# Long convolutions beside an MLP on TensorE: two blocks of 1024 with 32 by 32 point transforms in place of one 64 by 32 transform of 2048, and a new pacing

## The chip, the cores and the metric

The kernel runs on one core of a Trainium2 chip. The metric is device time in microseconds (us) of one execution, as a median over runs; lower is better. The program is a forward and backward pass with two branches on the same normalised input: a gated MLP and a long convolution. TensorE does the matrix products of both, VectorE and ScalarE the element-wise work, and one engine, SyncE, issues nearly all DMA transfers (1041 of 1121 in the kernel before).

## The reference, cut to what matters

```python
# branch A: k_shift = short causal filter of k (4 taps); kv = k_shift * v
kv_f = rfft(pad(kv, L=4096)); kf_f = rfft(pad(ssm_k, L=4096))   # per channel, 1024 channels
y = irfft(kv_f * kf_f)[:2048] + kv * ssm_D
out_A = q * y                                                    # q = layernorm(x)
# branch B: gated MLP, F = 3584
out_B = (relu(x @ W_gate) * (x @ W_up)) @ W_down
# result: x + out_A + out_B, and by autodiff the gradients of all inputs for a given grad_out
```

Per group of 128 channels automatic differentiation turns this into three forward transforms (filter H, gradient G, kv K), three products in the spectrum and three return transforms. There are eight groups.

## The kernel before

Each transform of 2048 points is made of a first stage R over 64 points, a 32 by 32 transpose on VectorE ("flip"), and a second stage FW over 32 points with the twiddles in its weights. The way back is IA, flip, RB. ScalarE copies each result from PSUM, where the matmuls put it, to SBUF, where the next stage reads it.

```python
def fwd1(self, st, key, src):                      # first stage, R
    B = st[key] = self.big.tile([P, 64, 2, 16, 2], BF16, name="B", tag="big")
    for r0 in range(0, 16, 8):
        for j in range(r0, r0 + 8, 4):
            ps = self.ps.tile([P, 2, 4, P], F32, name="ps1", tag="aps")      # pool of 2 buffers
            for u in range(2):
                rows = slice(64 * u, 64 * u + 64)
                self.mm(ps[:, u]..., self.R[rows]..., src[rows, j:j + 4, :]...)   # 64x128 of the array
            self.act(B[:, :, :, j:j + 4, :], ps[:]...)
        yield
# ... inv_b, the last stage, RB:
            for jj in range(2):
                for u in range(2):
                    n0 = 16 * u + 8 * j + 4 * jj
                    self.mm(ps[64 * u:64 * u + 64, 512 * jj:512 * jj + 512],
                            self.RB[:], Cf[:, n0:n0 + 4, :]...)                  # 128x64 of the array
# ... the product in the spectrum, per half:
            self.tt(t1[:], X[:, g], Z[:, g], ALU.mult)                 # 2048 elements
            self.tt(t2[:, 0], X[:, g, 0], Z[:, g, 1], ALU.mult)        # 1024 each
            self.tt(t2[:, 1], X[:, g, 1], Z[:, g, 0], ALU.mult)
            self.tt(Q[:, g, 0], ...); self.tt(Q[:, g, 1], ...)
```

The convolution is a list of small steps, each at most one burst of matmuls, one piece of VectorE work, or one set of loads. They are woven into the MLP by a budget in nanoseconds of MLP matmul time:

```python
SLOT = 1760
# in steps():
            for p, d in self.slots(st, gi):       # p: a burst or a set of loads; d: VectorE work
                self.run(p); self.run(d)
                yield self.SLOT
# among the slots: next_1 loads the next group's filter, gradient and xn; next_2 its k, v and taps
# the driver, after each run of eight MLP matmuls (ns = 1730):
                left -= ns * pace
                while a_steps is not None and left <= 0:
                    d = next(a_steps, None)
                    ...
                        left += d
```

In the MLP's hidden layer the weights of the next block of 512 columns are fetched late in the current one, into buffers that the current block has just left (cut):

```python
            def gate_up(sp):
                for s in (sp, sp + 1): gate(s); yield from step()
                if end: load_gate()                 # four DMAs of 256 KB, on SyncE
                for s in (sp, sp + 1): up(s); yield from step()
                if end: load_up()
```

Of the kernel before, what the change touches and what calls it, by code (L numbers as in the profile page):

```python
# [48 lines left out]
class ABranch:  # L49
# [5 lines left out]
    def __init__(self, tc, pri, S, D, k, v, g, shift_k, ssm_k, ssm_D, xn_d, y_d, sk_d, out_gk, out_gv, out_gsk,  # L55
                 out_gh, out_gsD):
        assert S == 2048 and D % P == 0
        self.tc, self.nc, self.pri = tc, tc.nc, pri
        self.S, self.D, self.NG = S, D, D // P
        self.k, self.v, self.g, self.shift_k, self.ssm_k, self.ssm_D = k, v, g, shift_k, ssm_k, ssm_D  # L60
        self.xn_d, self.y_d, self.sk_d = xn_d, y_d, sk_d
        self.out_gk, self.out_gv, self.out_gsk, self.out_gh, self.out_gsD = out_gk, out_gv, out_gsk, out_gh, out_gsD
        self.pools, self.pin = [], False
# [51 lines left out]
    def tables(self):  # L115
# [5 lines left out]
        self.IA = con.tile([P, 16, 2, 2, NB1], BF16, name="IA")  # L121
        self.R = con.tile([P, 2, 2, NB1], BF16, name="R")
        self.RB = con.tile([P, 64], BF16, name="RB")
        self.gs_all = con.tile([P, self.NG, 4], F32, name="gs_all")
        self.gD_all = con.tile([P, self.NG], BF16, name="gD_all")
# [20 lines left out]
        n1 = pbit(63, 1.0, "n1p")  # L146

        def first(n, name):
            it = self.ts.tile([P, 2, 2, NB1], I32, name="it" + name, tag="ts")
            tr = self.ts.tile([P, 2, 2, NB1], F32, name="tr" + name, tag="ts")  # L150
            nc.gpsimd.iota(it[:], pattern=[[128, 2], [0, 2], [4, NB1]], base=1, channel_multiplier=0)
            for a in range(2):
                V.tensor_scalar(out=it[:, :, a, :], in0=it[:, :, a, :], scalar1=n[:], scalar2=64.0 * (1 + a) + 128.0,
                                op0=ALU.mult, op1=ALU.add)
            V.tensor_single_scalar(out=it[:], in_=it[:], scalar=255, op=ALU.bitwise_and)
            nc.scalar.activation(out=tr[:], in_=it[:], func=ACT.Sin, scale=TWO_PI / 256, bias=negpi[:])
            return tr

        V.tensor_copy(out=self.R[:], in_=first(n1, "R")[:])

        e128 = con.tile([P, 1], F32, name="e128")
        V.scalar_tensor_tensor(out=e128[:], in0=b64[:], scalar=128.0, in1=b5[:], op0=ALU.mult, op1=ALU.mult)
        itF = big.tile([P, NB1, NB1], I32, name="itF", tag="big")
        nc.gpsimd.iota(itF[:], pattern=[[4, NB1], [256, NB1]], base=1, channel_multiplier=0)
        for ri in range(2):
            off = lin(b32, -2048.0, 2048.0 * (1 + ri) + 4096.0, "offF%d" % ri)
            V.tensor_tensor(out=off[:], in0=off[:], in1=e128[:], op=ALU.add)
            q = big.tile([P, NB1, NB1], I32, name="qF", tag="big")
            V.tensor_scalar(out=q[:], in0=itF[:], scalar1=b5[:], scalar2=off[:], op0=ALU.mult, op1=ALU.add)
            V.tensor_single_scalar(out=q[:], in_=q[:], scalar=8191, op=ALU.bitwise_and)  # L170
            nc.scalar.activation(out=self.FW[:, :, ri, :], in_=q[:], func=ACT.Sin, scale=TWO_PI / 8192,
# [4 lines left out]
        k256 = lin(b5, 256.0, 0.0, "k256")  # L176
        V.scalar_tensor_tensor(out=q32[:], in0=q32[:], scalar=32.0, in1=k256[:], op0=ALU.mult, op1=ALU.add)
        wI = con.tile([P, 16, 1], F32, name="wI")
        itW = con.tile([P, 16, 1], I32, name="itW")
        nc.gpsimd.iota(itW[:].rearrange("p (e m) o -> p e (m o)", e=2), pattern=[[128, 2], [4, 8]], base=1,  # L180
                       channel_multiplier=0)
# [5 lines left out]
        prod = big.tile([P, 16, NB1], F32, name="prI", tag="big")  # L187
        V.tensor_tensor(out=prod[:], in0=wI[:].to_broadcast([P, 16, NB1]), in1=itN[:].to_broadcast([P, 16, NB1]),
                        op=ALU.mult)
        q = big.tile([P, 3, 16, NB1], I32, name="qI", tag="big")  # L190
        for z in range(3):
            V.tensor_scalar(out=q[:, z], in0=prod[:], scalar1=2048.0 * z + 4096.0, scalar2=None, op0=ALU.add)
        V.tensor_single_scalar(out=q[:], in_=q[:], scalar=8191, op=ALU.bitwise_and)
        for ri in range(2):
            for a in range(2):
                nc.scalar.activation(out=self.IA[:, :, ri, a, :], in_=q[:, 1 - a + ri], func=ACT.Sin,
                                     scale=TWO_PI / 8192, bias=negpi[:])

        kk = con.tile([P, 1], F32, name="kkB")
        k4 = lin(b5, 4.0, 1.0, "k4")  # L200
        V.scalar_tensor_tensor(out=kk[:], in0=b64[:], scalar=128.0, in1=k4[:], op0=ALU.mult, op1=ALU.add)
        ob = lin(b32, 64.0, 192.0, "obB")
        itB = con.tile([P, 64], I32, name="itB")
        nc.gpsimd.iota(itB[:], pattern=[[1, 64]], base=0, channel_multiplier=0)
        V.tensor_scalar(out=itB[:], in0=itB[:], scalar1=kk[:], scalar2=ob[:], op0=ALU.mult, op1=ALU.add)
        V.tensor_single_scalar(out=itB[:], in_=itB[:], scalar=255, op=ALU.bitwise_and)
        trB = con.tile([P, 64], F32, name="trB")
        nc.scalar.activation(out=trB[:], in_=itB[:], func=ACT.Sin, scale=TWO_PI / 256, bias=negpi[:])
        V.tensor_scalar(out=self.RB[:], in0=trB[:], scalar1=1.0 / 2048, scalar2=None, op0=ALU.mult)
# [37 lines left out]
    def load_filter(self, gi):  # L247
        cg = slice(gi * P, (gi + 1) * P)
        hn = self.ld.tile([P, 64, NB1], BF16, name="hn")
        for ch in range(2):  # L250
            c0 = gi * P + 64 * ch
            self.load(hn[64 * ch:64 * ch + 64], self.ssm_k[c0:c0 + 64, :].rearrange("c (q n) -> q c n", n=NB1))
# [64 lines left out]
    def fwd1_filter(self, st):  # L317

        B = st["Bh"] = self.big.tile([P, 2, 32, NB1, 2], BF16, name="B", tag="big")
        hn = st["hn"]  # L320
        for k0 in range(0, 4, 2):
            for k in range(k0, k0 + 2):
                ps = self.ps.tile([P, 2, 512], F32, name="ps0", tag="aps")
                for ch in range(2):
                    rows = slice(64 * ch, 64 * ch + 64)
                    self.mm(ps[:, ch], self.R[rows].rearrange("p e a l -> p (e a l)"),
                            hn[rows, 16 * k:16 * k + 16, :].rearrange("p c n -> p (c n)"))
                self.act(B[:, :, 8 * k:8 * k + 8],
                         ps[:].rearrange("p h (cp i n) -> p h cp n i", i=2, n=NB1))
            yield  # L330

    def add_D(self, st):
        for rows in (slice(0, 32), slice(64, 96)):
            b0 = st["Bh"][rows].rearrange("p h cp n i -> p (h cp) n i")[:, :, 0, :]
            self.tt(b0, b0, st["sD"][rows].rearrange("p (cp i) -> p cp i", i=2), ALU.add)

    def fwd1(self, st, key, src):
        B = st[key] = self.big.tile([P, 64, 2, 16, 2], BF16, name="B", tag="big")
        for r0 in range(0, 16, 8):
            for j in range(r0, r0 + 8, 4):  # L340
                ps = self.ps.tile([P, 2, 4, P], F32, name="ps1", tag="aps")
                for u in range(2):
                    rows = slice(64 * u, 64 * u + 64)
                    self.mm(ps[:, u].rearrange("p r c -> p (r c)"), self.R[rows].rearrange("p e a l -> p (e a l)"),
                            src[rows, j:j + 4, :].rearrange("p r c -> p (r c)"))
                self.act(B[:, :, :, j:j + 4, :], ps[:].rearrange("p u r (cp i) -> p cp u r i", i=2))
            yield

    def fwd2(self, st, key, flp):
        F, Bf = self.form(key), st[flp]  # L350
        st[key] = F
        for j0 in range(0, 4, 2):
            for j in range(j0, j0 + 2):
                ps = self.ps.tile([P, 2, 2, 2, P], F32, name="ps2", tag="aps")
                for ri in range(2):
                    for m in range(2):
                        for q in range(4):
                            for e in range(2):
                                rows, l = slice(64 * e, 64 * e + 64), 8 * q + 2 * j + m
                                self.mm(ps[32 * q:32 * q + 32, e, ri, m, :], self.FW[rows, l, ri, :], Bf[rows, l, :])  # L360
                self.act(F[:, 2 * j:2 * j + 2].rearrange("p e i c -> p (e i c)"),
                         ps[:].rearrange("p e i m c -> p (e i m c)"))
            yield

    def form(self, name):
        return self.frm.tile([P, 8, 2, 256], BF16, name=name, tag="frm")

    def cmul(self, st, x, z, conj, name):

        X, Z = st[x], st[z]  # L370
        Q = st[name] = self.form(name)
        for hf in range(2):
            g = slice(4 * hf, 4 * hf + 4)
            t1 = self.tmp.tile([P, 4, 2, 256], BF16, name="t1", tag="tmp")
            t2 = self.tmp.tile([P, 2, 4, 256], BF16, name="t2", tag="tmp")
            self.tt(t1[:], X[:, g], Z[:, g], ALU.mult)
            yield
            self.tt(t2[:, 0], X[:, g, 0], Z[:, g, 1], ALU.mult)
            yield
            self.tt(t2[:, 1], X[:, g, 1], Z[:, g, 0], ALU.mult)  # L380
            yield
            self.tt(Q[:, g, 0], t1[:, :, 0], t1[:, :, 1], ALU.add if conj else ALU.subtract)
            yield
            self.tt(Q[:, g, 1], t2[:, 0], t2[:, 1], ALU.subtract if conj else ALU.add)
            yield

    def inv_a(self, st, key, q_name):
        C = st[key] = self.big.tile([P, 64, 4, 8, 2], BF16, name="C", tag="big")
        Q = st[q_name]
        for j0 in range(0, 4, 2):  # L390
            ps = [self.ps.tile([P, 2, 2, 2, P], F32, name="ps3", tag="aps") for _ in range(2)]
            for j in range(2):
                for m in range(2):
                    for ri in range(2):
                        for q in range(4):
                            for e in range(2):
                                rows, x = slice(32 * q, 32 * q + 32), 8 * e + 2 * (j0 + j) + m
# [1081 lines left out]
```

## Time and profile before

| | before |
|---|---|
| median time | 1908.5 us of four runs (1907.3 to 1910.3) |
| TensorE busy | 1895.0 us, 100% of the span |
| VectorE / ScalarE busy | 48% / 32% |
| convolution's bursts on TensorE | 192, costing 141.3 us |

A row of a group has line, engine, operation, out<-in, shape and count, then busy us and mean ns of one, then the engine's idle time before them and what ended it. A row of the timeline has start and length in us. "PEld" is TensorE's loading of weights into the array, not from memory. The prediction shows the lines themselves.

### The profile page before, as it was taken

To read this page: it belongs to the slowest core of one execution; us is meant where nothing else is said; L and a number is where in the kernel's file an instruction comes from. 1 tells how busy PE (TensorE), PEld (TensorE's weight loads), DVE (VectorE), ACT (ScalarE), POOL (GpSimd) and SP (SyncE) were. 2 spreads that over 40 slices of the span, in tenths; PEclk is the share of its full clock that TensorE was granted. 3 is DMA by queue.
4 is the path that set the end of the run, shared out by engine and by line. 5 is a ranking of instruction groups with operands and counts; after the bars stand their busy time and mean duration, and the time that the engine had idled before them with its cause. 6 is when DMAs were issued, how large, how long until landed. Compare 5 with 4: busy or idle time off the path is not lost.

```text
span 1904.1 us, 36029 instructions
## 1 busy us (share of the span) xinstructions
PE 1895.0 (100%) x15447; PEld 871.9 (46%) x15447; DVE 910.1 (48%) x1355; ACT 618.2 (32%) x858; POOL 15.0 (1%) x37
## 2 busy tenths in 40 slices
PE   9999999999999999999999999999999999999999
PEld 4444444444444444444444444444444544444444
DVE  6667777777777764454354445400222232222222
ACT  5755445445345445344344354311000000000000
POOL 1000000000000000000000000000000000000000
PEclk9999999999999999999999999999999999999999
DMA  9897679877577773566562633394999964554553
GB/s 251 247 226 163 169 185 212 184 202 164 143 200 163 204 208 114 147 157 200 132 170 95 159 112 122 112 290 130 267 237 244 234 142 122 122 122 122 122 122 72
DMA packets 692641, 323.14 MB, mean 170 GB/s; under 512 B 524024, under 2 KB 663040, under 8 KB 692480
## 3 DMA queue, kind: packets, MB, share of 16 engines
q1 hardware_dynamic: 681984, 299.99, 63.4%
q10 hardware_dynamic: 9216, 16.65, 2.8%
q0 software_dynamic: 1280, 4.20, 0.6%
q8 instruction: 120, 1.97, 0.4%
q14 instruction: 41, 0.34, 0.1%
HBM read 143.79 MB, written 95.44 MB: 126 GB/s over the span
## 4 chain that ended last, share of the span: by engine, by line
PE 97%; DVE 1%; DMA 1%; issue 0%; SPq 0%; ACT 0%; DVEq 0%; ACTq 0%
PE ps_x L1336 20%; PE ps_w L1109 20%; PE ps_o L1267 10%; PE ps_h L852 10%; PE ps_u L852 10%; PE ps_g L852 9%; PE ps_d L1109 9%; PE ps L72 6%; PE ps_d L1122 1%; PE ps_w L1122 1%; DMA wg<-in_B_W_gate_dram 0%; PE ps_r L1297 0%; DMA wu<-in_B_W_up_dram 0%; SPq L88 0%; DVE ru L956 0%
## 5 line engine op out<-in xcount | busy, mean ns | idle before, releaser
L1109 PE MATMUL ps_w<-ugs,xn_nat 128*128 128x512 bf16 x1728 | 383.3, 379 | 0.0
L852 PEld LDWEIGHTS <-xnT 128*128 128x128 bf16 x1792 | 170.3, 98 | 209.8 <-issue 9.1
L1109 PEld LDWEIGHTS <-xn_nat 128*128 128x128 bf16 x1728 | 164.6, 98 | 200.6 <-issue 7.6
L852 PE MATMUL ps_g<-wg,xnT 128*128 128x512 bf16 x896 | 206.3, 379 | 1.5 <-ACT xnT L887 0.4
L852 PE MATMUL ps_u<-wu,xnT 128*128 128x512 bf16 x896 | 206.9, 379 | 0.0
L852 PE MATMUL ps_h<-wdT,goT 128*128 128x512 bf16 x896 | 205.6, 379 | 0.0
L1354 ACT ACTIVATE w<-xn,m 128x512 f32<-128x512 bf16 x32 | 24.3, 806 | 553.0 <-issue 317.2
L1336 PE MATMUL ps_x<-wgT,ggT 128*128 128x512 bf16 x896 | 198.6, 379 | 0.0
L1336 PE MATMUL ps_x<-wuT,guT 128*128 128x512 bf16 x896 | 198.6, 379 | 0.0
L1267 PE MATMUL ps_o<-wd,hT 128*128 128x512 bf16 (+1 forms) x896 | 187.6, 372 | 0.0
L1109 PE MATMUL ps_d<-g_nat,hs 128*128 128x512 bf16 x768 | 172.1, 379 | 0.0
L1336 PEld LDWEIGHTS <-guT 128*128 128x128 bf16 x896 | 87.7, 98 | 105.7
L1336 PEld LDWEIGHTS <-ggT 128*128 128x128 bf16 x896 | 87.7, 98 | 105.5
L314 DVE STREAM_TRANSPOSE flp<-C 128x1024 f32<-128x1024 f32 x48 | 90.1, 1934 | 91.8 <-ACT C L76 91.8
L1267 PEld LDWEIGHTS <-hT 128*128 128x128 bf16 x896 | 87.7, 98 | 99.9
L852 PEld LDWEIGHTS <-goT 128*128 128x128 bf16 x896 | 85.0, 98 | 104.7 <-issue 5.8
L956 DVE SCALAR_TENSOR_TENSOR ru<-ru,ps_u 128x512 bf16<-128x512 bf16 x112 | 76.6, 684 | 107.3 <-issue 45.1
L1025 ACT CAST gh<-ps_h 128x512 bf16<-128x512 f32 x112 | 65.5, 584 | 171.3 <-PE ps_h L852 162.9
L1213 ACT CAST wi<-ps_w 128x512 bf16<-128x512 f32 x108 | 63.7, 590 | 162.6 <-PE ps_w L1109 156.6
L76 ACT CAST C<-ps 128x1024 bf16<-128x1024 f32 x96 | 92.5, 1015 | 70.1 <-PE ps L72 68.9
L1109 PEld LDWEIGHTS <-hs 128*128 128x128 bf16 x768 | 72.3, 98 | 89.6 <-issue 5.9
L1338 DVE CUSTOM_DVE_ANT_0 gx<-ps_x,gy 128x512 f32<-128x512 f32 x32 | 22.1, 691 | 182.3 <-PE ps_x L1336 182.2
(160 smaller groups left out, 1495.2 us busy)
## 6 DMA issues: line engine op xcount, KB each, us to landing
ug_d<-ru SPq DMA_DIRECT2D x112, 256.0 KB
ugs<-ug_d SPq DMA_DIRECT2D x112, 256.0 KB
wg<-in_B_W_gate_dram SPq DMA_DIRECT2D x56, 256.0 KB
wu<-in_B_W_up_dram SPq DMA_DIRECT2D x56, 256.0 KB
h_d<-ht SPq DMA_DIRECT2D x112, 128.0 KB
hs<-h_d SPq DMA_DIRECT2D x56, 256.0 KB
out_dram<-wi SPq DMA_DIRECT2D x56, 256.0 KB
gt<-in_grad_out_dram SPq DMA_DIRECT2D x32, 256.0 KB
```

Of the source, the lines that this page charges most:

```text
L72: self.pri.pin(self.nc.tensor.matmul(out, lhsT=lhsT, rhs=rhs, start=start, stop=stop))
L76: self.pri.pin(self.nc.scalar.copy(out=out, in_=in_))
L314: self.pri.pin(self.nc.vector.transpose(out=df[:, c0:c0 + 32, :], in_=sf[:, c0:c0 + 32, :]))
L852: self.pri.pin(self.nc.tensor.matmul(ps[:], lhsT=xT[:, kt * P:(kt + 1) * P], rhs=w(kt), start=(kt == 0), stop=(kt == self.DT - 1)), always ...
L956: self.pri.pin(nc.vector.scalar_tensor_tensor(out=ru[s][:, 1, :], in0=ru[s][:, 0, :], scalar=0.0, in1=ps[:], op0=ALU.is_gt, op1=ALU.mult))
L1025: self.pri.pin(nc.scalar.copy(out=gh[:], in_=ps[:]))
L1109: self.pri.pin(self.nc.tensor.matmul(ps[:], lhsT=lhsT(st), rhs=rhs(st), start=(st == 0), stop=(st == self.ST - 1)))
L1122: self.pri.pin(self.nc.tensor.matmul(ps[i][:], lhsT=lhsT(i, st), rhs=rhs(i, st), start=(st == 0), stop=(st == self.ST - 1)))
L1213: self.pri.pin(nc.scalar.copy(out=wo[0][:, d, :], in_=ps[:]))
L1267: nc.tensor.matmul(ps, lhsT=hT[:, kt, :], rhs=self.wd[:, kt, oc], start=(kt == 0), stop=(kt == self.FT - 1))
L1336: nc.tensor.matmul(ps, lhsT=T[:, kt, :], rhs=W[:, kt, oc], start=(i == 0), stop=(i == n - 1))
L1354: nc.scalar.activation(out=w[:, oc], in_=xn[:, oc], func=ACT.Identity, scale=m[:, 7:8], bias=m[:, 6:7])
```

## The change

The intent is to split each transform of 2048 into two blocks of 1024, so that the first and the last stage have 32 points where they had 64. Their matmuls then fit smaller tiles of the array, eight of which can work side by side (in the kernel before, the first eight matmuls of each FW burst, on 64 by 32 tiles, start within 24 ns). The two blocks are put together again in the spectrum, which costs VectorE more work ("turn" and a longer product). The pacing was changed with it. The core, with cuts:

```diff
-    SLOT = 1760
+    SLOT, DENSE = 1900, (1760, 1250)
...
-                yield self.SLOT
+                yield self.DENSE[p is None] if self.dense else self.SLOT   # dense: after the hidden layer
...
 def fwd1
-            for j in range(r0, r0 + 8, 4):
-                for u in range(2):
-                    rows = slice(64 * u, 64 * u + 64)
-                    self.mm(ps[:, u]..., self.R[rows] (64x128), src[rows, j:j + 4, :]...)
+            for u in range(2):
+                for b in range(2):
+                    rows = slice(64 * u + 32 * b, 64 * u + 32 * b + 32)
+                    for h in range(2):
+                        self.mm(ps[64 * h:64 * h + 64, b], self.R[rows] (32x64), src[rows, r0:r0 + 8, 64 * h:64 * h + 64])
 def inv_b
-                    self.mm(ps[64 * u:64 * u + 64, 512 * jj:512 * jj + 512], self.RB[:] (128x64), ...)
+            for q in range(4):
+                for e in range(2):
+                    rows, n0 = slice(64 * e, 64 * e + 64), 16 * (q // 2) + 8 * j
+                    self.mm(ps[32 * q:32 * q + 32, e], self.RB[rows, e, :] (64x32), ...)
+def turn: two additions of 1024 elements, in place, on the spectra G and H
 def cmul, per half
+                self.tt(t[i][:], M0, N[:, g, :, ::-1] if i else N[:, g], ALU.mult)      # 2048, twice
+                self.tt(u[:], M[:, g, 1], N[:, g, e, ::-1] if i else N[:, g, e], ALU.mult)
+                self.tt(t[i][:, :, f], t[i][:, :, f], u[:], ALU.add)                    # 1024, twice each
...
 def load_filter: four loads of 128 KB per group in place of two of 256 KB
 def store_gh: two stores of the filter's gradient per group in place of one
```

## The prediction

> **What bounds the kernel now.** I read the page of the profile first, its busy shares and its forty slices:
>
> ```profile
> PE 1895.0 (100%) x15447; PEld 871.9 (46%) x15447; DVE 910.1 (48%) x1355; ACT 618.2 (32%) x858; POOL 15.0 (1%) x37
> ...
> PE   9999999999999999999999999999999999999999
> ...
> DVE  6667777777777764454354445400222232222222
> ...
> PEclk9999999999999999999999999999999999999999
> ```
>
> TensorE is busy for 1895.0 of 1904.1 us, in every slice, at full granted clock. The time is therefore a sum of matmul time, and a change moves it in two ways only: by taking matmul time away, or by making TensorE wait. VectorE matters only through the second. The chain of waits says the same (PE 97% of the span). Its share "PE ps L72 6%" is the convolution: line 72 is the helper that issues its matmuls, in bursts between those of the MLP.
>
> I then split line 72 by form (columns: count, busy us, mean ns, idle before):
>
> ```profile
> L72 PE MATMUL ps<-flp,FW 64*32 64x128 bf16 x3072 | 36.2, 221 | 0.5 <-DVE flp L314 0.5
> ...
> L72 PE MATMUL ps<-flp,RB 128*64 128x512 bf16 x128 | 16.9, 385 | 0.0
> ...
> L72 PE MATMUL ps<-GKV,IA 32*64 32x128 bf16 x1024 | 12.4, 224 | 0.0
> ...
> L72 PE MATMUL ps<-gt,R 64*128 64x512 bf16 x64 | 9.7, 381 | 0.0
> ```
>
> "64*128" is the part of the array that one matmul takes (rows by columns). The forms 64*32 and 32*64 put eight matmuls side by side, 64*128 and 128*64 only two. The R form stands three times (inputs gt, kvt, hn). To price a burst I used the timeline, of one first-stage (R) and one last-stage (RB) burst:
>
> ```profile
> 133.45 1.90 PE L852 MATMUL ps_g<-wg,xnT 128*128 128x512 bf16 x8
> 135.28 0.61 PE L72 MATMUL ps<-gt,R 64*128 64x512 bf16 x4
> 135.82 3.63 PE L852 MATMUL ps_u<-wu,xnT 128*128 128x512 bf16 x16
> ...
> 196.20 2.54 PE L852 MATMUL ps_u<-wu,xnT 128*128 128x512 bf16 x11
> 198.66 1.05 PE L72 MATMUL ps<-flp,RB 128*64 128x512 bf16 x8
> 199.65 3.19 PE L852 MATMUL ps_h<-wdT,goT 128*128 128x512 bf16 x14
> ```
>
> MLP matmuls start 0.216 us apart (the median of consecutive starts in the trace), so the eighth of the first run started at 133.45 + 7 x 0.216 = 134.96. The next MLP matmul starts at 135.82. Less the one step of 0.216 that would have passed anyway, the burst costs 0.64 us. In the same way the RB burst costs 199.65 - 198.36 - 0.216 = 1.07 us. Over all bursts of a kind the medians are: R 0.633 us (48 bursts of 4 matmuls), RB 1.080 us (16 of 8), FW 0.776 us (48 of 64), IA 0.785 us (48 of 64). With the tap sums (8.8 us), the filter's last stage (7.4 us) and the halo (1.3 us) all 192 bursts cost 141.3 us; the rest of the 1904 is the MLP, which the change does not touch.
>
> The individual starts within a burst say what that cost is made of. In an R burst they are at 0, 3, 226 and 229 ns, with the last MLP start at -312 and the next at 538: two matmuls together, two more when these are through (about 216), and about 95 ns lost at the switch on either side. In an RB burst they are at 0, 3, 240, 243, 456, 459, 672, 675: four turns of two.
>
> [...] The trace has 3 to 4 ns: the first eight of an FW burst start at 0, 3, 6, 10, 13, 16, 20, 23, and the same holds for most IA bursts. This is the step on which the gain rests: eight tiles of 64*32 or 32*64 really run together here. [...] The trace agrees for plain operands (1216 ns for 2048 elements, 683 for 1024). The changed kernel reverses and repeats middle dimensions only, so I expect the same durations; no run here shows that form yet.
>
> **The change part by part.** The burst count stays at 192 in the built program, so no mode switch is saved.
>
> (a) First stage. A block of 1024 has 32 points where 64 stood, so R goes from 64*128 to 32*64: eight matmuls of 512 columns per burst in place of four, each in its own tile (four row groups by two column groups[...]). All eight should start within 24 ns. Cost: 309 into the burst + 24 + 308 out - 216 = 425 ns against 633. Saved: 48 x 0.208 = 10.0 us. The filter's bursts have the same form.
>
> (b) Last stage. RB goes from 128*64 to 64*32: sixteen matmuls per burst on eight tiles, two turns in place of four. Last start at about 229 + 24 = 253 ns. Cost: 309 + 253 + 308 - 216 = 654 against 1080. Saved: 16 x 0.426 = 6.8 us.
>
> (c) FW, IA and the filter's last stage keep count and size; only their access patterns change. 0.
>
> (d) VectorE gets more work, since the recombination is done in the spectrum. Rows used:
>
> ```profile
> L314 DVE STREAM_TRANSPOSE flp<-B 128x1024 f32<-128x1024 f32 x48 | 90.7, 1937 | 37.4 <-ACT B L76 37.0
> ...
> L80 DVE TENSOR_TENSOR t<-H,G 128x1024 bf16<-128x1024 bf16 x32 | 20.9, 683 | 0.0
> ...
> L80 DVE TENSOR_TENSOR t<-H,G 128x2048 bf16<-128x2048 bf16 x16 | 19.4, 1213 | 31.5 <-ACT G L76 31.5
> ```
>
> Counted in the built program: 48 more products of 2048 elements (58 us), 96 additions of 1024 that are new (66 us; the 96 products of 1024 and the 96 closing additions replace as many), and 32 operations of 1024 for the two turns per group (22 us). Together +146 us, to about 1055 us or 55%. It lies beside TensorE as long as results are there in time.
>
> (e) Pacing. The convolution's 568 steps are spread over MLP matmuls, formerly one per 1.76 us of MLP time; now one per 1.9 while the hidden layer runs (VectorE serves the MLP there too), then one per 1.76 or 1.25. In the built order the convolution ends 272 MLP matmuls earlier (4833 against 5105), 59 us. It was not on the path, but the weights of the output phase load after it, so nothing gets later there.
>
> ScalarE's copies keep count and size, and DMA bytes are the same.
>
> Sum: 1909.6 - 16.8 = 1892.8 us if TensorE waits no more than before.
>
> **Waits, the first rival.** VectorE's load by stage of the kernel before (stretch, its length, then busy us of each engine):
>
> ```profile
> 400.00:780.00 380.00, 379.55 (x3982) 174.03 (x3981) 254.52 (x314) 180.36 (x238) 0.82 (x2) 1.00 0.67 172
> ...
> 1000.00:1243.00 243.00, 243.00 (x2516) 112.09 (x2515) 109.44 (x113) 101.01 (x133) 0.41 (x1) 1.00 0.42 124
> ```
>
> That is 67% while the hidden layer runs and 45% after. With the added work and the new pace I sum about 77% and 57%. On average there is room, but [...]one stretch of each later group is tight: from the flip of K to the return transform of GKV there are 12 steps of 1.25 and 6 of 1.76 us, with five bursts of 0.78, so about 29.5 us of TensorE time. In it VectorE has four flip halves (7.2 at 1.8 from start to start), about 15 product steps of 1.2 (18), a turn (1.2) and a gate product (1.1): about 27.5, or 93%. Steps come in lumps of eight MLP matmuls (1.73 us), so now and then a burst will find its flip 0.1 to 1.5 us late. With some five late groups and one or two such places each I put down 2.5 us, an estimate from these sums. So: 1892.8 + 2.5, about 1895 us.
>
> **Other rivals.** The 32*64 tiles may not run side by side with 512 columns[...]: then (a) gives nothing, and the first stage costs its 633 ns as before: 1905 us. Against it stands that IA already runs eight at once with 128 columns. [...] A third: fewer slots during the hidden layer relieve DMA and PSUM and remove small waits. But TensorE's idle time before MLP matmuls is only some 3 us, nearly all at the start: at most 1 us.
>
> **Range and chances.** If the stagger is larger than 3 ns the gain falls by 1 or 2 us; waits may be 0 or 10 us. That gives 1887 to 1904. Faster by 2% means below 1871, more than twice the time that the two stages can give; slower by 2% means above 1948, which needs waits of 55 us[...]. So within 2% is nearly certain.
>
> **What would show it.** In the changed profile: R bursts with starts within 24 ns and a cost near 0.43 us; RB bursts near 0.65; FW and IA bursts unchanged near 0.78; 192 bursts costing about 124.5 us together; products of 2048 elements still near 1216 ns; VectorE busy near 1055 us; idle time before line 72's matmuls, released by VectorE's flips, of a few us. I am wrong if R bursts still show a second turn at 226 ns, if the reversed products take 2.3 us, or if TensorE's idle time grows by more than 10 us.

## The result, and the profile after

The changed kernel took 1907.37 us (median of four, 1906.47 to 1908.53), the kernel before 1908.47. The ratio is 0.9994, with a 95% interval of 0.9976 to 1.0011: the same. I had predicted 1895, with 1887 to 1904 as the range, so the prediction was wrong.

The page of the changed kernel, busy shares:

```profile
PE 1866.1 (98%) x15525; PEld 870.7 (46%) x15768; DVE 1047.8 (55%) x1528; ACT 616.2 (32%) x858; POOL 14.9 (1%) x37
```

TensorE's busy time is 29 us less, yet the time is the same. Part of that is a gap in the record: there are 15,768 weight loads but 15,525 matmuls, one of which belongs to each weight load, so 243 matmuls are missing. In the kernel before both counts are 15,447. A burst or a wait next to a missing record looks longer than it is, so for sums over the whole span I use the starts of the weight loads, which are complete.

Groups of the changed kernel on TensorE, by form (the convolution's helper is still line 72; the MLP's gate and up products, line 852 before, are line 865 now):

```profile
L865 PE MATMUL ps_g<-wg,xnT 128*128 128x512 bf16 x865 | 206.9, 384 | 11.1 <-DMA wg<-in_B_W_gate_dram 8.2 <-issue 0.9 <-ACT xnT L900 0.4
L865 PE MATMUL ps_u<-wu,xnT 128*128 128x512 bf16 x863 | 204.8, 381 | 5.7 <-DMA wu<-in_B_W_up_dram 2.6 <-issue 1.9
...
L72 PE MATMUL ps<-flp,FW 64*32 64x128 bf16 x3072 | 36.6, 223 | 1.2 <-DVE flp L307 1.2
...
L72 PE MATMUL ps<-flp,RB 64*32 64x512 bf16 x256 | 10.0, 382 | 0.0
...
L72 PE MATMUL ps<-gt,R 32*64 32x512 bf16 x128 | 7.3, 397 | 0.1
```

The stages did what was hoped: RB went from 16.9 to 10.0 us and the R form of the gradient from 9.7 to 7.3. The loss stands in the first two rows: before its gate and up products TensorE now waits 8.2 and 2.6 us for weights to land. In the kernel before, the gate row had 1.5 us of idle time in all and the up row none.

The timeline has both, the gain and the loss. First a last-stage burst and what followed it, then a first-stage burst:

```profile
236.85 3.63 PE L865 MATMUL ps_g<-wg,xnT 128*128 128x512 bf16 x15
240.41 0.62 PE L72 MATMUL ps<-flp,RB 64*32 64x512 bf16 x16
243.49 4.82 PE L865 MATMUL ps_u<-wu,xnT 128*128 128x512 bf16 x14 [2.45 <-DMA wu<-in_B_W_up_dram]
...
636.49 1.89 PE L865 MATMUL ps_g<-wg,xnT 128*128 128x512 bf16 x8
638.31 0.42 PE L72 MATMUL ps<-kvt,R 32*64 32x512 bf16 x8
638.67 1.69 PE L865 MATMUL ps_g<-wg,xnT 128*128 128x512 bf16 x7
```

The R burst lasts 0.42 us where it lasted 0.61, the RB burst 0.62 where it lasted 1.05. But after that RB burst TensorE stands still for 2.45 us until the up weights are there. The worst case is at 617 us. TensorE, then the queue of the issuing engine SyncE ("SPq"), both of the changed kernel:

```profile
616.15 1.67 PE L865 MATMUL ps_h<-wdT,goT 128*128 128x512 bf16 x7 [0.16 <-issue]
622.37 3.95 PE L865 MATMUL ps_g<-wg,xnT 128*128 128x512 bf16 x10 [4.55 <-DMA wg<-in_B_W_gate_dram]
```

```profile
607.94 4.42 SPq L88 DMA_DIRECT2D hn<-in_A_ssm_k_dram  x4
612.46 2.84 SPq L88 DMA_DIRECT2D gt<-in_grad_out_dram  x2
615.34 0.66 SPq L88 DMA_DIRECT2D sD<-in_A_ssm_D_dram  x1
616.05 1.32 SPq L88 DMA_DIRECT2D xt<-xn_d  x2
617.48 2.81 SPq L858 DMA_DIRECT2D wg<-in_B_W_gate_dram  x4
```

For 9.5 us SyncE does nothing but issue the convolution's loads for its next group, and the gate weights stand behind them. The same four loads of weights in the kernel before:

```profile
607.53 1.38 SPq L863 DMA_TRANSPOSE wdT<-in_B_W_down_dram  x1
609.00 0.55 SPq L1030 DMA_DIRECT2D ug_d<-ru  x1
609.64 2.38 SPq L845 DMA_DIRECT2D wg<-in_B_W_gate_dram  x4
```

There they were issued at 609.6 to 611.6 us and used at 619.2, with 7.6 us to spare. I looked at this for all blocks of the hidden layer (counted from 0): the time to spare is the span from the last issue of a block's weights to the moment when TensorE was ready for them, that is, to the end of the matmul before. In the changed kernel three have too little, and these are where TensorE waits: up 5 has 0.3 us, gate 7 has 0.1, and gate 13 has less than nothing, since its last weights were issued 2.0 us after TensorE was ready. All other weights have about 4 us or more. In the kernel before, the least are gate 8 with 2.3 and gate 11 with 2.5 us, where it waits 1.6 us in all.

A set of the convolution's loads stands directly ahead of the weights of up 5 and of gate 13. At gate 7 it stands 25 us ahead (issued from 296.4 to 306.0 us), but SyncE has no gap from there to the weights, which it issues at 330.9 us. In the kernel before, the same set was issued from 281.9 to 293.7 us and the weights at 325.7.

These waits cost more than their length: 26 MLP matmuls ran longer at half clock, 5.2 us in all (table below). The granted clock in four stretches of the changed kernel (stretch, its length, busy us of the engines, then clock, DMA share and GB/s):

```profile
622.40:625.70 3.30, 3.30 (x8) 1.17 (x9) 0.00 (x0) 0.00 (x0) 0.00 (x0) 0.50 1.09 358
626.00:640.00 14.00, 13.79 (x197) 6.35 (x198) 6.67 (x10) 9.38 (x13) 0.00 (x0) 1.00 0.83 271
```

Right after the wait at 617 us TensorE runs at half its clock (0.50 in the first row, 1.00 in the second). The clock records have such stretches of 3.41 us after the waits at 241 and 617 us and of 6.83 us at 336, and none in the kernel before, save at its end.

The sums, from the starts of weight loads (the excess over 0.216 us per step, changed kernel less kernel before):

| | us |
|---|---|
| R bursts | -6.7 |
| RB bursts | -7.0 |
| FW bursts (0.8 of it in one at half clock, the rest late flips) | +1.7 |
| other bursts | -0.1 |
| waits of MLP matmuls, nearly all for weights (12.2 against 2.3) | +10.0 |
| 26 MLP matmuls longer at half clock, most by 0.21 us | +5.2 |
| the rest | -0.1 |
| sum | +3.0 |

The two profiled spans differ by 2.6 us (1906.7 against 1904.1). So little is missing: the stages' gain of 13.7 us is there, and was paid back elsewhere.

### The profile page after: what moved, and what is told of

Its sections match the earlier page's. It is cut to its first block, busy times and chain, and to the rows that moved or that the text cites. A ratio compares the mean times of both kernels' runs of the same rounds, so it can differ in the third digit from the quotient of the medians.

```text
span 1906.7 us, 36606 instructions
## 1 busy us (share of the span) xinstructions
PE 1866.1 (98%) x15525; PEld 870.7 (46%) x15768; DVE 1047.8 (55%) x1528; ACT 616.2 (32%) x858; POOL 14.9 (1%) x37
## 4 chain that ended last, share of the span: by engine, by line
PE 93%; DMA 3%; issue 2%; DVE 1%; SPq 1%; ACT 0%; POOL 0%; DVEq 0%; POOLq 0%; ACTq 0%
PE ps_x L1349 20%; PE ps_w L1122 19%; PE ps_o L1280 10%; PE ps_u L865 9%; PE ps_g L865 9%; PE ps_h L865 9%; PE ps_d L1122 8%; PE ps L72 5%; PE ps_d L1135 1%; DMA wg<-in_B_W_gate_dram 1%; DMA wu<-in_B_W_up_dram 1%; PE ps_w L1135 0%; SPq L88 0%; DMA ugs<-ug_d 0%; DMA skb<-sk_d 0%
## 5 line engine op out<-in xcount | busy, mean ns | idle before, releaser
L1122 PE MATMUL ps_w<-ugs,xn_nat 128*128 128x512 bf16 x1670 | 375.4, 379 | 5.5 <-issue 3.8
L1122 PE MATMUL ps_d<-g_nat,hs 128*128 128x512 bf16 x735 | 167.4, 379 | 4.0 <-issue 3.0
L1272 DVE TENSOR_TENSOR ya<-ya,xe 128x1024 bf16<-128x1024 bf16 x16 | 11.1, 692 | 255.4 <-DMA xe<-xn_d 255.4
```

The lines of the kernel that those rows point to most:

```text
L1122: self.pri.pin(self.nc.tensor.matmul(ps[:], lhsT=lhsT(st), rhs=rhs(st), start=(st == 0), stop=(st == self.ST - 1)))
```

## The experiments

**The theories.** Queue theory: the new pacing moved the convolution's sets of loads within the program, three of these sets now stand ahead of MLP weights in SyncE's order, and TensorE waits for them. Rival 1: VectorE's added 138 us makes its results late, the stores of these results hold SyncE up, and so the weights are late. Rival 2: the filter's loads are issued in four pieces instead of two, and SyncE takes longer over them (1.45 us for each of the four against 2.2 for each of the two, so 1.4 us more per group).

**e1_hold_after.** The changed kernel with its new pacing; only the sets of loads are put off from some time before the MLP's weights to just after them.

```diff
+ self.hold = swap or sp >= 4      # late in a block of the hidden layer; in the two blocks that also fetch
+                                  # the next half's inputs (swap): throughout
  ... load_up(); + self.hold = False
- self.run(p)
+ if name in ("next_1", "next_2"): self.pend.append(p)     # a set of loads
+ else: self.run(p)                # the pending sets go first when hold is off, and before their first use at the latest
```

> The changed kernel; only the issue of the convolution's input loads (filter, gradient, xn; k, v, taps) is put off while the MLP is about to issue its next weights. Queue theory (these loads stand ahead of weight loads in the one in-order issue queue, and TensorE waits about 15 us): the three waits for weights at 241, 332 and 617 us go, time about 1894 us (1890 to 1898). Rival 1 (VectorE's extra 138 us makes its results and the stores behind them late, and these hold up the queue): time stays at 1905 to 1909. Rival 2 (the filter's loads cost more since they are four, not two): only part returns, 1900 to 1905.

Measured: 1895.74 us (1895.37 to 1896.17), ratio 0.9943 (0.9930 to 0.9955). SyncE's queue in the same place:

```profile
601.44 2.08 SPq L876 DMA_DIRECT2D wg<-in_B_W_gate_dram  x4
...
606.28 2.89 SPq L876 DMA_DIRECT2D wu<-in_B_W_up_dram  x4
609.22 3.86 SPq L89 DMA_DIRECT2D hn<-in_A_ssm_k_dram  x2
```

The filter's loads now come after both weights. Gate 13 has 7.7 us to spare, up 5 has 6.6 and gate 7 has 5.6; the three waits and the half clock are gone (mean granted clock 1.000). VectorE's work and the four pieces are untouched, so neither rival alone can be the cause of what came back, about 10 us (the ratio fell from 0.9994 to 0.9943).

Putting off has its own price, which I had not foreseen. After one of the two blocks in which the loads are held throughout, xn (the tile xt) lands late. VectorE waits for it and then has several operations in a row, and TensorE waits for VectorE:

```profile
348.26 1.23 DVE L81 TENSOR_TENSOR gt<-gt,xt 128x2048 bf16<-128x2048 bf16 x1 [6.07 <-DMA xt<-xn_d]
...
353.74 1.89 PE L883 MATMUL ps_g<-wg,xnT 128*128 128x512 bf16 x8 [1.81 <-DVE ru L989]
```

With a second wait of 0.5 us at 356 us this costs 2.3 us. No such wait stands there in the changed kernel or in e5.

**e2_hold_before.** The same edit in the kernel before.

> The kernel before with the same putting off of the convolution's input loads. Queue theory: it loses only about 1.6 us to late weights, so 1906 to 1908.5 us; the gain of the first run must not appear here. If it falls by more than 5 us, the kernel before paid for its queue order too and the first run says less about the change.

Measured: 1905.23 us, ratio 0.9992 (0.9979 to 1.0004). That is 0.8 us below the range expected, but the interval of the ratio includes 1: the kernel before had next to nothing to win from it.

**e3_newpace_before.** The kernel before with `SLOT, DENSE = 1900, (1760, 1250)` and nothing else.

> The kernel before, old transforms and old VectorE work, with the changed kernel's pacing alone (steps 1900 in the hidden layer, then 1760 or 1250). Its loads then stand in the same order among the weight loads as in the changed kernel. Queue theory: it pays the same waits and none of the gain: 1917 to 1924 us. Rival 1 (VectorE) and rival 2 (four loads): no loss, 1906 to 1911.

Measured: 1916.98 us (1915.62 to 1918.07), ratio 1.0054 (1.0042 to 1.0067). The old transforms, with VectorE's old load and the filter in two pieces, now wait at the same three places. TensorE at 617 us, as above:

```profile
616.17 1.67 PE L852 MATMUL ps_h<-wdT,goT 128*128 128x512 bf16 x7 [0.16 <-issue]
622.25 2.31 PE L852 MATMUL ps_g<-wg,xnT 128*128 128x512 bf16 x5 [4.41 <-DMA wg<-in_B_W_gate_dram]
```

Up 5 has 1.5 us to spare, gate 7 has 0.8, and gate 13's last weights were issued 1.8 us after TensorE was ready. The time is at the lower end of what the queue theory had (1917). The pacing alone makes the waits; both rivals predicted no loss here and fall.

**e4_oldpace_after.** The changed kernel with `SLOT, DENSE = 1760, (1760, 1760)`.

> The changed kernel with the old pacing (every step 1760). Its loads stand where they stood in the kernel before. Queue theory: most of the late weights go, 1892 to 1898 us, perhaps with 1 to 3 us of bursts that wait for VectorE. Rival 1 (VectorE): VectorE's load in the hidden layer rises from 77% to about 83%, so 1908 or more.

Measured: 1893.67 us (1891.62 to 1896.16), ratio 0.9931 (0.9918 to 0.9945). This is the transform change on its own, with the filter's loads in four pieces. What is left of late weights is 2.8 us at blocks 7, 8 and 11; the kernel before had 1.6 us, at 8 and 11.

**e5_oldpace_hold.** Both: the old pacing and the loads put off.

> The changed kernel with the old pacing and with the convolution's input loads put off: meant to beat both kernels. The old pacing leaves about 2.2 us of waits around weights 7, 8 and 11; if these were the queue's too, they go: 1889 to 1893 us, about 1.5 to 2 us under the old pacing alone (1893.7). If what is left over is VectorE, no gain over 1893.7.

Measured: 1893.01 us (1891.43 to 1895.82), ratio 0.9921 (0.9909 to 0.9933). It beats the kernel before by 0.8% and, by the ratios, the changed kernel by 0.7%. Whether it beats e4 can't be said: the runs of each spread over 4 us and the intervals overlap. In its profile one wait for weights of 0.7 us is left in the hidden layer (at gate 7), its bursts cost 14.4 us less than those of the kernel before, and the median is 14.9 us lower than that kernel's in the same rounds (1907.94).

**e6_old_last_stage.** e4 with RB in its old form, eight matmuls of 128 by 64 (wrong numbers).

> The changed kernel with the old pacing, but the last stage in its old form: eight matmuls of 128*64 per burst in place of sixteen of 64*32 (the numbers come out wrong on purpose). If the stage's gain of 0.43 us in each of 16 bursts reaches the time in full: 1893.7 + 6.8 = 1900.5 us (1899 to 1902). If TensorE's gain is eaten elsewhere: below 1897.

Measured: 1903.06 us (1900.00 to 1905.60), ratio 0.9974 (0.9962 to 0.9987). The difference of the ratios to e4 is 0.0043, or 8 us. That is 1 us above the range expected. In the profiles the bursts of the last stage cost 7.7 us more than in e4. The intervals of the two ratios leave the 8 us uncertain by some 3 us; within that, a microsecond of bursts is a microsecond of the kernel.

**e7_short_product.** e4 with the old product and no turns (wrong numbers).

> The changed kernel with the old pacing, with the old product (five operations a half) and no turns (wrong numbers on purpose): VectorE's added 138 us taken away, all else kept. If VectorE's work lies beside TensorE: 1891.5 to 1894 us, at most 2 us under 1893.7. If it costs on the path: 1889 or less.

Measured: 1893.05 us (1892.32 to 1896.40), ratio 0.9928 (0.9914 to 0.9941). Taking VectorE's added 138 us away changes nothing that can be told from the spread. At the old pacing that work lies beside TensorE's, to within some 3 us.

**e8_pace_2100.** The changed kernel with 2100 in place of 1900 in the hidden layer, chosen from the built order because it puts sets of loads ahead of other weights.

> The changed kernel with a slower pace in the hidden layer (2100 for 1900), which gives VectorE less to do per time but puts the filter, gradient and xn loads right ahead of gate weights 7 and the k and v loads ahead of gate and up weights 9. Queue theory, from the built order alone: the waits at weights up 5 and gate 13 go, a new one of 3 to 8 us comes at gate 7 (near 330 us) and a small one at 9; 1897 to 1905 us. If VectorE's load were the cause: faster than 1897, and no wait at gate 7 larger than before.

Measured: 1914.70 us (1912.74 to 1916.09), ratio 1.0033 (1.0020 to 1.0047). The places were right in the main, the size was not. Up 5 is in time. Block 13 still waits, 1.1 us for its gate weights and 1.4 for its up weights, in place of 4.9. TensorE waits at gate 7 and for 2.3 us at gate 9:

```profile
327.99 0.75 PE L72 MATMUL ps<-flp,FW 64*32 64x128 bf16 x64
333.94 0.59 PE L865 MATMUL ps_g<-wg,xnT 128*128 128x512 bf16 x1 [5.20 <-DMA wg<-in_B_W_gate_dram]
```

What I had not looked for in the order is a third place, 5.1 us at 672 us. A set of loads (issued from 658.6 to 670.2 us) stands there ahead of the operands of the next phase, not of weights. A slower pace for VectorE made the kernel slower by 7 us, which rival 1 can't have.

**e9_loads_gpsimd and e10_loads_scalar.** The changed kernel with its own pacing; `nc.sync.dma_start` becomes `nc.gpsimd.dma_start` or `nc.scalar.dma_start` in the convolution's load helper. Both were to tell the issuing engine from the 16 DMA engines behind it.

> The changed kernel with its new pacing and the same program order; only the convolution's input loads are issued by GpSimd's queue (idle 99% of the time) in place of SyncE's. The bytes, the 16 DMA engines and VectorE's work are the same. Queue theory in its narrow form (the issuing sequencer's order and time are what delays the weights): the three waits for weights go, 1892 to 1898 us. If the wait comes from the 16 DMA engines being busy with the convolution's small packets at that time: the waits stay, 1904 to 1909. If GpSimd prepares these many small rows too slowly, the convolution itself will wait and the time rises above 1910; then this run decides nothing.

Measured for e9: 1910.92 us (1905.69 to 1917.01), ratio 1.0014 (0.9997 to 1.0030). A miss, and over 1910 us, where by what I had written the time decides nothing. The profile (of the slowest run, 1917.01) says more. The weights are issued in time again: up 5, gate 7 and gate 13 have 6.5, 3.0 and 7.7 us to spare. But they land late all the same. TensorE's idle time put down to up weights is 4.9 us and to gate weights 4.0, against 2.6 and 8.2 in the changed kernel. The last-stage burst before up 5 is again followed by a wait:

```profile
255.49 1.31 PE L865 MATMUL ps_u<-wu,xnT 128*128 128x512 bf16 x4 [1.14 <-DMA wu<-in_B_W_up_dram]
```

The first of these weights landed 10.2 us after its issue, against 5.2 us in the changed kernel and 4.4 in the kernel before; GpSimd had issued the k and v loads just before, from 240.6 to 245.8 us. In block 13 the last piece of the gate weights landed 11.6 us after its issue, and TensorE waited 2.3 us for it. Other waits come on top, for the gradient and for the filter:

```profile
L865 PE MATMUL ps_h<-wdT,goT 128*128 128x512 bf16 x868 | 203.9, 382 | 5.3 <-DMA goT<-in_grad_out_dram 2.6 <-issue 1.7
...
L72 PE MATMUL ps<-hn,R 32*64 32x512 bf16 x128 | 9.9, 410 | 3.9 <-DMA hn<-in_A_ssm_k_dram 3.8
```

So the narrow form of the queue theory, in which only the issuing engine's order and time count, fails here: weights that are issued in time can still land late. That the convolution's loads ahead of the weights make the three waits is shown by e1 and e3. How much of that is SyncE's time and how much slow landing can only be estimated: in the changed kernel's trace the fastest weights land 3.0 us after their issue. The first piece of up 5 was issued 2.8 us before TensorE was ready for it, that of gate 13 only 0.3 us before. By this estimate some 0.2 of the 2.45 us at up 5 and some 2.6 of the 4.55 at gate 13 are late issue, and the rest slow landing.

> The same, but issued by ScalarE, which also evicts PSUM. Queue theory: the weights come in time again, but ScalarE loses 9 us of issuing per group of loads and any wait for a free buffer in the middle of its evictions: waits for PSUM appear, 1895 to 1908 us, with no idle time of TensorE put down to gate or up weights over 1 us.

Measured for e10: 1983.18 us (1974.86 to 1984.05), ratio 1.0384 (1.0368 to 1.0400). A miss by 75 us. Gate weights are waited for 0.6 us in all and up weights 0.9, as expected, but TensorE now waits for ScalarE's evictions, 40.0 us for those of H alone:

```profile
L72 PE MATMUL ps<-flp,FW 64*32 64x128 bf16 x3072 | 39.0, 230 | 40.0 <-ACT H L76 40.0
```

That these evictions stand behind loads that wait for free buffers in ScalarE's own order is my reading of it. What is measured is how long such loads waited in e9: GpSimd stood idle for 45.9 us before the filter's loads and for 8.4 us before the gradient's (at 606 and 619 us), until matmuls of the convolution had ended. If the reading is right, work stands behind waiting loads once more, this time on an engine that TensorE waits for.

## Why the prediction was wrong, point by point

**What bounds the kernel** held: the time is TensorE's busy time plus its waits, and e6 shows the first half of that directly.

**Step (a), the first stage**, was right in mechanism, but a third of its gain did not come. In 38 of the 48 bursts all eight matmuls start within 24 ns, as foreseen. The burst then costs 0.447 us instead of 0.425, since the next MLP matmul starts 331 ns after the last start, not 308. In the other 10 the second four were held back, by 0.05 to 0.38 us, most often 0.24: the PSUM pool has two buffers, and with a burst only one MLP run earlier ScalarE's copy of the previous result ended 0.2 us after the burst had begun. Together 6.7 us instead of 10.0. e4 and e5 have 7.7.

**Step (b), the last stage**, was right: 0.651 us per burst against 0.654 predicted, 7.0 us against 6.8.

**Step (c)**, no change in FW and IA: right (medians 0.987 and 0.996 us against 0.986 and 0.995, by weight-load starts).

**Step (d), VectorE**, was right. Busy time rose to 1047.8 us, against about 1055. That the reversed products would take as long as plain ones was an estimate of mine; only plain operands had been measured. They do: 1214 ns on average for 48 of them, against 1213 for the 48 others of the same size, with which they share a row (32 products each):

```profile
L80 DVE TENSOR_TENSOR t<-t,u 128x1024 bf16<-128x1024 bf16 x96 | 66.4, 692 | 3.3
...
L80 DVE TENSOR_TENSOR t<-H,G 128x2048 bf16<-128x2048 bf16 x32 | 38.2, 1219 | 0.1
L80 DVE TENSOR_TENSOR t<-K,G 128x2048 bf16<-128x2048 bf16 x32 | 37.8, 1212 | 0.0
```

**The first rival**, late flips, was too large and in the wrong place. Predicted were 2.5 us in the later groups. Measured are 0.9 us more, 0.7 of them in the first group (at 129 us) and none after 780 us.

**Step (e), pacing**, is the step that failed. I wrote that "nothing gets later there" and looked only at the end of the convolution. The pacing also sets where the convolution's loads stand among the MLP's in SyncE's one order, and three sets came to stand where they made weights late: two directly ahead of them, and one 25 us ahead of gate 7's in a stretch in which SyncE has no time left over. The third of the other rivals pointed the wrong way: it let fewer steps "relieve DMA" by at most 1 us, where the runs show a loss of about 15. With it fell the clause on which the sum rested, "if TensorE waits no more than before". The built order, which I had used to count bursts, already showed it: the k and v loads between gate 5 and up 5, the filter's right ahead of gate 13. Of the three observations by which I said I would be wrong, one came true, if narrowly: TensorE's idle time grew by more than 10 us (10.0 of waits and 0.9 of late flips). With the old pacing (e4) the prediction of 1895 would have been 1.3 us off, in part by luck: there the first stage gave 2.3 us less than predicted, and the late flips cost less too, 0.8 us.

Not the cause, by the runs: the tiles not running side by side (the starts), the reversed operands (the durations), VectorE's load (e3, e7), the four pieces of the filter (e3). Settled: the waits are made by where the convolution's loads stand among the weights (e1, e3, e4, e8). Open: how much of a late weight is SyncE's time and how much the transfer itself (e9).

## What to carry to other kernels

When a kernel weaves two streams of work together by a budget, changing the budget moves every load of both streams in the issuing engine's order (the new pacing alone cost the kernel before some 10 us, e3); before believing in a gain, list for each operand of the bounding engine how long before its use it is issued, and what stands ahead of it. Here 2.5 spare microseconds were a little too few (gate 11 of the kernel before) and 5.6 were enough (gate 7 in e1); but look at what else is in flight as well, since 6.5 were not enough in e9, where the weights took 10.2 us to land. A set of loads that is not urgent can be put off past the urgent ones, which left the results at the two paces within 4 us of each other (e1 and e5), but not past its own first use (2.3 us in e1). Moving it to another engine's queue did not help (1910.9 us in e9, 1983.2 in e10).

## Also measured

- Issuing took a large part of a transfer's time: a 128 KB piece of the filter took SyncE 1.45 us on average to issue, a third of the 4.4 us from issue to landing (median), and a set of nine loads held SyncE for 9.5 us.
- A wait of 2.45 us (at 241 us in the changed kernel) was followed by a stretch of 3.41 us at half clock. Not every such wait was: in e3 TensorE waited 2.6 us in all for up weights, and its up products took 379 ns on average, as in the kernel before; in the changed kernel, also with 2.6 us, they took 381. What made the difference is not shown.
- Products of 2048 16-bit elements with a repeated middle dimension in one operand and a reversed one in the other took 1214 ns on average, the same as plain ones in the kernel before (1213 to 1216).
